# A decode-attention kernel without its block, and one semaphore for both copies of an output row

## The chip, the cores and the metric

The kernel runs on one core of a Trainium2 chip. The core has five engines that run their own instruction streams and wait for each other through semaphores: TensorE (PE in the profile; its weight loads are PEld), VectorE (DVE), ScalarE (ACT), GpSimd (POOL) and SyncE (SP). Transfers between HBM and the core's memory are issued by an engine and carried by 16 DMA engines. A semaphore is a counter: an instruction or a landed transfer adds to it, and an instruction can wait until it has reached a value.

The metric is the device time of one execution in microseconds (us). Before the change it was 247.52 us, the median of 3 runs from 247.37 to 247.62.

## The reference

Two attention layers, A and B, each with one new token, are computed on inputs of their own, and their output rows are joined. Each has 32 query heads, 16 key and value heads (so two query heads share one), 8192 cached positions and a head size of 128. Layer A looks at the last 2048 positions alone, layer B at all 8192.

```python
W = min(4096, max(256, Sk // 4))          # A: 2048
q = (x @ wq).reshape(B, Sq, Hq, Dh)...    # x: 1 x 576
k = jnp.repeat(k_cache[:, :, Sk - W:, :], rep, axis=1)      # B: the whole cache
v = jnp.repeat(v_cache[:, :, Sk - W:, :], rep, axis=1)
scores = jnp.einsum("bhqd,bhkd->bhqk", q, k) * (Dh ** -0.5)
p = _softmax(scores, axis=-1)
o = jnp.einsum("bhqk,bhkd->bhqd", p, v)
return o.transpose(0, 2, 1, 3).reshape(B, Sq, Hq * Dh) @ wo
...
return jnp.concatenate([a, b], axis=-1)   # 1 x 1 x 1152, bf16
```

## The kernel before

The work is the reading of the caches and weights, some 103 MB, each byte used once or twice. All large loads go into one ring buffer, `ring`, in a fixed order that SP issues: the query weights of both layers, then keys and values in eight units (four of layer A, four of layer B, each with four key heads), then the output weights, the last of which come in five pieces of falling size. A load into a part of the ring waits until the work that read this part before is done.

For each unit, DVE transposes the keys slab by slab (`ktb`, line 363), PE multiplies them with the queries (`score`, line 380), the maximum is taken and spread (`peak`, `spread`), ACT makes the exponentials (`expo`, line 419), DVE transposes them (`turnp`), and PE multiplies them with the values (`pv`, line 444). The transposing and scoring of the next unit are put between the softmax steps of the present one. After the last unit the sums are divided out, and the output projection (line 523) makes, for layer A and then layer B, one row of 576 numbers in two pieces of 320 and 256. ACT copies the first piece from PSUM (line 531), DVE the second (line 533), and SP sends the row out (line 535).

The program is written through the class `Prog`. Its methods `op` and `load` only append to a list for each engine; a dependency is the name of an earlier operation. An operation that others depend on adds 1 to its engine's own semaphore (`prog_act`, `prog_dve` and so on). A load adds 16 to a semaphore of its own. `emit` then walks through each engine's list and, ahead of each operation, puts a wait for every semaphore that the engine has not yet seen reach the wanted value (`eng.wait_ge`, line 83). Of several waits ahead of one instruction, the last is carried by the instruction itself and the ones before it stand as instructions of their own, which the profile shows as event semaphores.

`emit` hands each engine's list to a block: `with nc.Block() as block: pg.emit(block)`, lines 538 and 539, with a function for each of the five engines (`@block.sync` and so on). A block gives each engine a part of the program of its own, to which the engine goes from the main body. At the block's end every engine drains, adds to a common semaphore, and waits until POOL, which counts the others, lets all of them go. In the profile the instructions of the block's end stand on line 539. Those on line 554, where the program is opened, are memsets of constants and a barrier of the same kind, ahead of everything else. SP's list ends with an empty instruction that waits until both output rows have landed.

Of the kernel before, what the change touches and what calls it, by code (L numbers as in the profile page):

```python
# [8 lines left out]
ACT = mybir.ActivationFunctionType  # L9
# [5 lines left out]
DM = 576  # L15
# [14 lines left out]
N0 = 320  # L30
# [6 lines left out]
class Prog:  # L37
# [9 lines left out]
    def op(self, eng, fn, deps=(), name=None):  # L47
        self.ops[eng].append((fn, tuple(deps), name, None))
        if name is not None:
            assert name not in self.where, name  # L50
            self.where[name] = (eng, len(self.ops[eng]) - 1)

    def load(self, eng, fn, sem, value, deps=(), name=None):
        self.ops[eng].append((fn, tuple(deps), None, sem))
        if name is not None:
            assert name not in self.dma, name
            self.dma[name] = (sem, value)

    def emit(self, block):
        used = set()  # L60
        for ops in self.ops.values():
            for _, deps, _, _ in ops:
                used.update(d for d in deps if d not in self.dma)
        value = {}
        for e, ops in self.ops.items():
            n = 0
            for _, _, name, _ in ops:
                if name in used:
                    n += 1
                    value[name] = (self.sem[e], n, e)  # L70

        def run(e, eng):
            seen = {}
            for fn, deps, name, dsem in self.ops[e]:
                need = {}
                for d in deps:
                    s, v = self.dma[d] if d in self.dma else value[d][:2]
                    key = id(s)
                    if v > need.get(key, (None, 0))[1]:
                        need[key] = (s, v)  # L80
                for key, (s, v) in need.items():
                    if v > seen.get(key, 0):
                        eng.wait_ge(s, v)
                        seen[key] = v
                ins = fn(eng)
                if dsem is not None:
                    ins.then_inc(dsem, 16)
                elif name in used:
                    ins.then_inc(self.sem[e], 1)

        @block.sync
        def _(eng):
            run("sp", eng)

        @block.gpsimd
        def _(eng):
            run("pool", eng)

        @block.tensor
        def _(eng):  # L100
            run("pe", eng)

        @block.vector
        def _(eng):
            run("dve", eng)

        @block.scalar
        def _(eng):
            run("act", eng)


def bass_concat_heads__sliding_block_cached__gqa_block_cached__decode_kernel(nc, A_x, A_k_cache, A_v_cache, A_wq, A_wo,
# [47 lines left out]
    outsb = nc.alloc_sbuf_tensor("outsb", [1, 2 * DM], BF16)  # L160
# [10 lines left out]
    pg = Prog(nc)  # L171
    op, load = pg.op, pg.load
    s_x = [nc.alloc_semaphore("s_x%d" % i) for i in range(2)]
    s_ld = [nc.alloc_semaphore("s_ld%d" % i) for i in range(NSEM)]
    s_out = nc.alloc_semaphore("s_out")


    live, at, nload, uses_of = [], [0], [0], []

    def place(size, uses, issue, name):  # L180
        if at[0] + size > RING:
            at[0] = 0
        lo, hi = at[0], at[0] + size
        at[0] = hi
        deps = []
        for r in list(live):
            if r[0] < hi and lo < r[1]:
                deps += r[2]
                live.remove(r)
        n = nload[0]  # L190
        nload[0] += 1
        if n >= NSEM:
            deps += uses_of[n - NSEM]
        uses_of.append(list(uses))
        live.append((lo, hi, list(uses)))
        t = ring[:, lo:hi]
        load("sp", lambda e: issue(e, t), s_ld[n % NSEM], 16 * (n // NSEM + 1), deps=deps, name=name)
        return t
# [47 lines left out]
    def slab(kind, i, s):  # L246
# [10 lines left out]
       deps=["id0"], name="ident")  # L257
# [6 lines left out]
    for P in range(2):  # L264
        x = xs[P]
        load("act", lambda e, x=x, P=P: e.dma_start(
            xrow[0:1, P * DM:(P + 1) * DM], bass.AP(tensor=x.tensor, offset=x.offset, ap=[[DM, 1], [1, DM]])),
            s_x[P], 16, name="x%d" % P)
# [4 lines left out]
    for c in range(2):  # L273
        op("dve", lambda e, c=c: e.tensor_reduce(par[:, c:c + 1], view(identf, 128, c, [[2, 64]]), AX.X, ALU.add),
           deps=["identf"], name="par%d" % c)
# [3 lines left out]
    for P in range(2):  # L279
# [3 lines left out]
        for k in range(5):  # L283
            def mm(e, P=P, k=k):
                if k < 4:
                    lhsT = view(xrow, 2 * DM, P * DM + k, [[4, 128]], parts=1)
                else:
                    lhsT = xdup[0:1, P, :]
                return e.matmul(banks[2 * P + k // 4][:, (k % 4) * 128:(k % 4 + 1) * 128], lhsT=lhsT,  # L289
                                rhs=onesb[0:1, :], start=True, stop=True)  # L290
# [3 lines left out]
        for c in range(2):  # L294
            op("dve", lambda e, P=P, c=c: e.tensor_scalar(
                xrep[:, P, 4 + c, :], banks[2 * P + 1][:, 0:128], par[:, c:c + 1], None, ALU.mult),
                deps=["xT%d.4" % P, "par%d" % c], name="xr%d.%d" % (P, 1 + c))
# [3 lines left out]
       deps=["identf"], name="clsb")  # L301
    op("dve", lambda e: e.tensor_reduce(clsa[:], view(identf, 128, 0, [[1, 8], [8, 16]]), AX.X, ALU.add),
       deps=["identf"], name="clsa")
    op("dve", lambda e: e.tensor_reduce(sel[:], view(identf, 128, 0, [[1, 32], [32, 4]]), AX.X, ALU.add),
       deps=["identf"], name="sel")
# [6 lines left out]
    for P in range(2):  # L312
        for n in range(8):
# [3 lines left out]
            def mm(e, P=P, n=n, bank=bank):  # L317
# [8 lines left out]
               name="qmm%d.%d" % (P, n))  # L326
            op("act", lambda e, u=u, bank=bank: e.activation(qsb[:, u % 4, :], bank[:, :], ACT.Copy),  # L327
               deps=["qmm%d.%d" % (P, n)] + (["qT%d" % (u // 2 - 2)] if u >= 4 else []), name="qe%d" % u)
            if n % 2:
# [3 lines left out]
                    deps=["qe%d" % (u - 1), "qe%d" % u] + (["z0.%d" % i for i in range(4)] if P else []),  # L333
                    name="qT%d" % (u // 2))
        for b in range(4):
            if P == 1:
# [3 lines left out]
                    deps=["qT%d" % u for u in range(4, 8)] + ["zb0"], name="z1.%d" % b)  # L340
            else:
# [3 lines left out]
                    deps=["qT%d" % u for u in range(4)] + ["za0"], name="z0.%d" % b)  # L345
# [122 lines left out]
    for i in range(NU):  # L468
# [34 lines left out]
       deps=["lsel", "lselA", "nb%d" % last, "mr%d" % last], name="L")  # L503
# [3 lines left out]
        deps=["rl", "O%d" % last], name="on")  # L507
    op("dve", lambda e: e.transpose(oq[:].rearrange("p c k -> p (c k)"), on[:].rearrange("p c k -> p (c k)")),
       deps=["on"], name="oq")
# [5 lines left out]
    fb = qb[0]  # L515
    for P in range(2):
        k0 = 0
        for c, kk in enumerate(NWO[P]):
            def mm(e, P=P, c=c, k0=k0, kk=kk):
                for k in range(kk):  # L520
                    for n in range(2):
                        r, lo, hi = 32 * (2 * P + n), n * N0, N0 + n * (DM - N0)
                        ins = e.matmul(fb[r:r + 1, 0:hi - lo], lhsT=oP[:, P, k0 + k:k0 + k + 1],  # L523
                                       rhs=wo_at[P, c][:, k * DM + lo:k * DM + hi],
                                       start=(k0 + k == 0), stop=(k0 + k == HQ - 1))
                return ins
            op("pe", mm, deps=["wo%d.%d" % (P, c), "oP", "exp%d" % (NQ - 2)], name="F%d.%d" % (P, c))
            k0 += kk
        done = "F%d.%d" % (P, len(NWO[P]) - 1)
        r, lo = 64 * P, P * DM  # L530
        op("act", lambda e, r=r, lo=lo: e.activation(outsb[0:1, lo:lo + N0], fb[r:r + 1, 0:N0], ACT.Copy),
           deps=[done], name="f%d.0" % P)
        op("dve", lambda e, r=r, lo=lo: e.tensor_copy(outsb[0:1, lo + N0:lo + DM], fb[r + 32:r + 33, 0:DM - N0]),  # L533
           deps=[done], name="f%d.1" % P)
        load("sp", lambda e, lo=lo: e.dma_start(out[0, 0:1, lo:lo + DM], outsb[0:1, lo:lo + DM]),
             s_out, 16 * (P + 1), deps=["f%d.0" % P, "f%d.1" % P], name="out%d" % P)
    op("sp", lambda e: e.nop(), deps=["out1"])

    with nc.Block() as block:
        pg.emit(block)  # L540


# [26 lines left out]
```

## Time and profile before

| | before |
|---|---|
| median of 3 runs | 247.52 us (247.37 to 247.62) |
| the profiled execution | 247.68 us |
| its span, first to last instruction of the trace | 245.5 us |
| instructions | 2266 |
| PE / DVE / ACT / POOL busy | 71% / 53% / 10% / 3% of the span |
| HBM read | 102.76 MB, 419 GB/s over the span |
| mean granted TensorE clock | 0.805 |

The profile is that of one execution. Its time is longer than its span, since the execution also has parts before the first and after the last instruction of the program, which the trace does not hold. An engine's name with a q (SPq) stands for instructions that its sequencer handles alone: waits, branches, drains and the issuing of DMAs. These are not counted as busy. A row such as `L539 SPq DRAIN x1: 7/7/7, 245.3 to 245.3` gives the line, the engine, the instruction and how many, the shortest, median and longest duration in ns, and the start of the first and the last of them in us. In the chain of work and in the timeline each row begins with the start and the duration in us. In the table of waits a row gives who waited for whom, the total in us, how often, and the longest.

### The profile page before, as it was taken

Reading aid. Unit: us, or ns where it says so; the run is one execution under the profiler, and the core shown is the slowest. Engines: PE = TensorE matmul, PEld = TensorE weight load, DVE = VectorE, ACT = ScalarE, POOL = GpSimd, SP = SyncE. Lnnn points to the kernel's source line nnn. Section 1 sums busy time; section 2 is a strip of 40 time slices with the busy share of each in tenths; the row PEclk is TensorE's granted clock in tenths of the full one; section 3 lists DMA queues with packets and bytes.
Section 4 is the critical chain, followed back from the end, with each engine's and each line's share of the span. In section 5 each row is a group of like instructions: output and inputs, shape, how many; then the busy total and the mean of one; then the engine's idle time right before and its main releaser. Section 6 shows DMA issues by size and latency. Waiting matters only on the chain.

```text
span 245.5 us, 2266 instructions
## 1 busy us (share of the span) xinstructions
PE 174.3 (71%) x960; PEld 73.5 (30%) x961; DVE 129.5 (53%) x162; ACT 24.3 (10%) x52; POOL 8.2 (3%) x15
## 2 busy tenths in 40 slices
PE   0269958789769995799371979946679939338396
PEld 0124423234433323332030523212423203214263
DVE  0423447786878986799301699810689910500200
ACT  2005530101201000100000100000010000100001
POOL 8400000000000000000000000000000000000000
PEclk9999997797995999579859559977558976875569
DMA  7999999999999999998999999899999999999993
GB/s 272 415 450 413 441 430 424 427 427 456 428 435 392 472 427 427 446 470 384 406 432 435 459 448 470 384 411 440 432 460 448 406 395 435 427 444 426 412 408 144
DMA packets 4482, 102.90 MB, mean 419 GB/s; under 512 B 501, under 2 KB 633, under 8 KB 1145
## 3 DMA queue, kind: packets, MB, share of 16 engines
q1 hardware_dynamic: 4468, 102.76, 97.8%
q8 instruction: 7, 0.11, 0.2%
q14 instruction: 3, 0.02, 0.0%
q10 hardware_dynamic: 4, 0.00, 0.0%
HBM read 102.76 MB, written 0.00 MB: 419 GB/s over the span
## 4 chain that ended last, share of the span: by engine, by line
DMA 70%; PE 20%; DVE 8%; issue 1%; SPq 1%; ACT 0%; DVEq 0%
DMA ring<-in_B_v_cache_dram 39%; DMA ring<-in_B_wo_dram 13%; DMA ring<-in_B_k_cache_dram 12%; PE vb L444 8%; DVE ktb L363 7%; DMA ring<-in_A_wq_dram 5%; PE sb L323 4%; PE qb L323 3%; PE sb L380 3%; PE qb L523 1%; SPq L242 0%; PE ob L460 0%; DVE ktb L330 0%; DVE zb L337 0%; ACT qsb L327 0%
## 5 line engine op out<-in xcount | busy, mean ns | idle before, releaser
L363 DVE STREAM_TRANSPOSE ktb<-ring 128x1024 int32<-128x1024 int32 x80 | 92.9, 1212 | 30.1 <-DMA ring<-in_B_k_cache_dram 29.4
L380 PE MATMUL sb<-ktb,zb 128*128 128x512 bf16 x256 | 76.7, 445 | 21.8 <-DVE ktb L363 19.5
L380 PEld LDWEIGHTS sb<-ktb,zb 128*128 128x128 bf16 x256 | 24.1, 108 | 70.8 <-DVE ktb L363 41.8
L444 PE MATMUL vb<-ring,pts 128*32 128x512 bf16 x256 | 24.8, 568 | 20.5 <-DMA ring<-in_B_v_cache_dram 16.4
L380 PE MATMUL qb<-ktb,za 128*128 128x512 bf16 x64 | 20.2, 466 | 1.5 <-DVE ktb L363 1.5
L444 PEld LDWEIGHTS vb<-ring,pts 128*32 128x32 bf16 x256 | 8.9, 135 | 35.5 <-DMA ring<-in_B_v_cache_dram 18.5
L451 ACT ACTIVATE xo<-vb 128x512 f32<-128x512 f32 x8 | 4.8, 597 | 131.8 <-PE vb L444 131.8
L431 DVE STREAM_TRANSPOSE pts<-psb 32x512 bf16<-32x512 bf16 x16 | 11.3, 703 | 8.6 <-ACT psb L419 8.4
L330 DVE STREAM_TRANSPOSE ktb<-qsb 128x512 int32<-128x512 int32 x8 | 5.7, 711 | 14.7 <-ACT qsb L327 14.7
L323 PE MATMUL sb<-ring,xrep 128*128 128x512 bf16 x40 | 11.4, 441 | 2.9 <-DMA ring<-in_A_wq_dram 2.5
L523 PE MATMUL qb<-ring,oP 128*1 128x256 bf16 (+1 forms) x128 | 11.1, 333 | 3.0 <-DMA ring<-in_A_wo_dram 2.8
L460 PEld LDWEIGHTS ob<-sel,xo 128*128 128x128 f32 x64 | 11.6, 260 | 3.8 <-ACT xo L451 2.4
L460 PE MATMUL ob<-sel,xo 128*128 128x8 f32 x64 | 11.0, 299 | 1.2 <-ACT xo L451 1.2
L380 PEld LDWEIGHTS qb<-ktb,za 128*128 128x128 bf16 x64 | 6.4, 112 | 12.3 <-issue 6.3
L323 PE MATMUL qb<-ring,xrep 128*128 128x512 bf16 x39 | 9.1, 379 | 0.0
L523 PEld LDWEIGHTS qb<-ring,oP 128*1 128x1 bf16 x128 | 6.7, 92 | 7.3 <-DMA ring<-in_A_wo_dram 2.9
L504 DVE RECIPROCAL rl<-mb 128x64 f32<-128x64 f32 x1 | 0.6, 558 | 14.0 <-PE mb L501 14.0
L533 DVE CAST outsb<-qb 1x256 bf16<-1x256 f32 x2 | 0.8, 420 | 13.4 <-PE qb L523 13.4
L289 PE MATMUL sb<-onesb,xrow 1*128 1x128 bf16 x4 | 0.6, 295 | 9.2 <-DVE xdup L280 9.2
L405 DVE TENSOR_REDUCE mr<-mb 1x8 f32<-1x128 f32 x8 | 1.9, 241 | 9.4 <-PE mb L397 9.4
L323 PEld LDWEIGHTS sb<-ring,xrep 128*128 128x128 bf16 x40 | 4.2, 108 | 8.9 <-issue 5.6
L327 ACT ACTIVATE qsb<-sb 128x512 bf16<-128x512 f32 x8 | 4.8, 598 | 19.2 <-PE sb L323 18.5
(65 smaller groups left out, 69.5 us busy)
## 6 DMA issues: line engine op xcount, KB each, us to landing
ring<-in_B_k_cache_dram SPq DMA_DIRECT2D x8, 4096.0 KB, 25.3
ring<-in_A_k_cache_dram SPq DMA_DIRECT2D x4, 2048.0 KB, 30.9
ring<-in_A_v_cache_dram SPq DMA_DIRECT2D x4, 2048.0 KB, 26.2
ring<-in_B_v_cache_dram SPq DMA_DIRECT2D x2, 4096.0 KB, 24.1
ring<-in_A_wo_dram SPq DMA_DIRECT2D x1, 4608.0 KB, 24.4
ring<-in_A_wq_dram SPq DMA_DIRECT2D x1, 4096.0 KB, 12.4
ring<-in_B_wq_dram SPq DMA_DIRECT2D x1, 4096.0 KB, 22.4
ring<-in_B_wo_dram SPq DMA_DIRECT2D x1, 2448.0 KB, 29.9
```

The lines of the kernel that those rows point to most:

```text
L323: ins = e.matmul(bank[:, :], lhsT=lhsT, rhs=o, start=(k == 0), stop=(k == 4))
L327: op("act", lambda e, u=u, bank=bank: e.activation(qsb[:, u % 4, :], bank[:, :], ACT.Copy), deps=["qmm%d.%d" % (P, n)] + (["qT%d" % (u // ...
L330: op("dve", lambda e, u=u, n=n: e.transpose(ktb[:, (n - 1) * 512:(n + 1) * 512].bitcast(I32), qsb[:, u % 4 - 1:u % 4 + 1, :].rearrange("p ...
L363: op("dve", lambda e: e.transpose(kt.bitcast(I32), src.bitcast(I32)), deps=[landed] + (["S%d" % (k - NKT)] if k >= NKT else Z), name="T%d. ...
L380: ins = e.matmul(bank[:, :], lhsT=lhsT, rhs=view(ktb, KT, (k % NKT) * SLAB + 64 * c + v, [[128, 16], [2, 32]]), start=(side == "B" and s = ...
L405: op("dve", lambda e: e.tensor_reduce(out, view(mb, 512, 0, rows, parts=1), AX.X, ALU.max), deps=deps, name="mr%d" % i)
L431: op("dve", lambda e, b=b: e.transpose(view(pts, NB * 128, 2 * b, [[8, 16], [128, NB], [1, 2]], 32, 32 * b), psb[32 * b:32 * b + 32, :]), ...
L444: ins = e.matmul(vbank[i][32 * j:32 * j + 32, :], lhsT=lhsT, rhs=src[:, 512 * j:512 * j + 512], start=(s == 0), stop=(s == nslab[i] - 1))
L451: op("act", lambda e: e.activation(xo[:, c, :], vbank[i][:, :], ACT.Copy), deps=["V%d.%d" % (i, nslab[i] - 1)] + (["O%d" % (i - 1)] if i e ...
L460: ins = e.matmul(ob[:, at:at + 8], lhsT=xo[:, c, 128 * t:128 * t + 128], rhs=sel[:, 8 * t:8 * t + 8], start=(t == 0), stop=(t == 3))
L523: ins = e.matmul(fb[r:r + 1, 0:hi - lo], lhsT=oP[:, P, k0 + k:k0 + k + 1], rhs=wo_at[P, c][:, k * DM + lo:k * DM + hi], start=(k0 + k == 0 ...
L533: op("dve", lambda e, r=r, lo=lo: e.tensor_copy(outsb[0:1, lo + N0:lo + DM], fb[r + 32:r + 33, 0:DM - N0]), deps=[done], name="f%d.1" % P)
```

## The change

There are two parts. The block is gone: `emit` calls the same function for each engine in turn on the engines of the main body, so that the instructions follow the opening barrier directly and nothing of the block's end stands behind them. SP's list ends with a wait alone: an operation without a function puts out its waits and nothing more. And the two copies of an output row, one by ACT and one by DVE, each add 1 to a semaphore of that row, `s_row[P]`; the row's DMA waits for the value 2, where it waited for DVE's and for ACT's own semaphore.

```diff
-    def load(self, eng, fn, sem, value, deps=(), name=None):
-        self.ops[eng].append((fn, tuple(deps), None, sem))
+    def load(self, eng, fn, sem, value, deps=(), name=None, step=16):
+        self.ops[eng].append((fn, tuple(deps), None, (sem, step)))
...
-    def emit(self, block):
+    def emit(self):
...
+                if fn is None:
+                    continue
                 ins = fn(eng)
                 if dsem is not None:
-                    ins.then_inc(dsem, 16)
+                    ins.then_inc(*dsem)
...
-        @block.sync
-        def _(eng):
-            run("sp", eng)
-
-        @block.gpsimd
-        def _(eng):
-            run("pool", eng)
...
+        for e, eng in (("sp", self.nc.sync), ("pool", self.nc.gpsimd), ("pe", self.nc.tensor),
+                       ("dve", self.nc.vector), ("act", self.nc.scalar)):
+            run(e, eng)
...
+    s_row = [nc.alloc_semaphore("s_row%d" % i) for i in range(2)]
...
-        op("act", lambda e, r=r, lo=lo: e.activation(outsb[0:1, lo:lo + N0], fb[r:r + 1, 0:N0], ACT.Copy),
-           deps=[done], name="f%d.0" % P)
-        op("dve", lambda e, r=r, lo=lo: e.tensor_copy(outsb[0:1, lo + N0:lo + DM], fb[r + 32:r + 33, 0:DM - N0]),
-           deps=[done], name="f%d.1" % P)
+        load("act", lambda e, r=r, lo=lo: e.activation(outsb[0:1, lo:lo + N0], fb[r:r + 1, 0:N0], ACT.Copy),
+             s_row[P], 2, deps=[done], name="f%d" % P, step=1)
+        load("dve", lambda e, r=r, lo=lo: e.tensor_copy(outsb[0:1, lo + N0:lo + DM], fb[r + 32:r + 33, 0:DM - N0]),
+             s_row[P], 2, deps=[done], step=1)
         load("sp", lambda e, lo=lo: e.dma_start(out[0, 0:1, lo:lo + DM], outsb[0:1, lo:lo + DM]),
-             s_out, 16 * (P + 1), deps=["f%d.0" % P, "f%d.1" % P], name="out%d" % P)
-    op("sp", lambda e: e.nop(), deps=["out1"])
-
-    with nc.Block() as block:
-        pg.emit(block)
+             s_out, 16 * (P + 1), deps=["f%d" % P], name="out%d" % P)
+    op("sp", None, deps=["out1"])
+
+    pg.emit()
```

More of the change, by code (lines that the diff above doesn't have):

```diff
@@ L84, in run @@
                         seen[key] = v
+                if fn is None:
+                    continue
                 ins = fn(eng)
                 if dsem is not None:
-                    ins.then_inc(dsem, 16)
+                    ins.then_inc(*dsem)
                 elif name in used:
                     ins.then_inc(self.sem[e], 1)
-        @block.sync
-        def _(eng):
-            run("sp", eng)
-        @block.gpsimd
-        def _(eng):
-            run("pool", eng)
[L99 to L109, printed above, removed]
+        for e, eng in (("sp", self.nc.sync), ("pool", self.nc.gpsimd), ("pe", self.nc.tensor),
+                       ("dve", self.nc.vector), ("act", self.nc.scalar)):
+            run(e, eng)
 def bass_concat_heads__sliding_block_cached__gqa_block_cached__decode_kernel(nc, A_x, A_k_cache, A_v_cache, A_wq, A_wo,
```

## The prediction

> **What bounds the kernel now.** I read the busy line and the slices first, then the DMA queues, the chain that ended last, the records of the two lines outside the work (554, where the program is opened, and 539, where the block ends), and SP's waits.
>
> ```profile
> span 245.5 us, 2266 instructions
> PE 174.3 (71%) x960; PEld 73.5 (30%) x961; DVE 129.5 (53%) x162; ACT 24.3 (10%) x52; POOL 8.2 (3%) x15
> DMA  7999999999999999998999999899999999999993
> HBM read 102.76 MB, written 0.00 MB: 419 GB/s over the span
> ```
>
> No engine is busy for much more than 71% of the span, while the DMA engines are full in all slices but the first and the last. The kernel reads 102.76 MB and is bound by that reading. The change touches no load, so it can only act on the two ends, where the DMA engines are not full: the start, before the first load is under way, and the end, after the last load has landed. The chain of work shows both.
>
> ```profile
> 0.67 0.06 issue
> 0.73 0.41 SPq L205
> 1.14 0.06 issue
> 1.20 13.18 DMA ring<-in_A_wq_dram
> ...
> 36.57 4.64 DVE ktb L363 x4
> 41.20 0.02 issue
> 41.22 29.23 DMA ring<-in_B_k_cache_dram
> ...
> 92.14 1.01 PE vb L444 x16
> 93.15 0.02 issue
> 93.17 0.02 SPq L83
> 93.18 0.03 issue
> 93.21 30.75 DMA ring<-in_B_v_cache_dram
> ...
> 242.86 0.66 PE qb L523 x5
> 243.51 0.02 issue
> 243.54 0.43 ACT outsb L531
> ```
>
> SP issues the first load at 0.73. At the other end PE's last product of the output projection is done at 243.51 and the copy of the second output row at 243.54 + 0.43 = 243.97. The chain is cut there, but the span goes on to 245.5: 1.5 us for the output's DMA and the end of the program.
>
> ```profile
> 244.04 0.25 SPq L535 DMA_DIRECT2D out_dram<-outsb  x1
> ...
> SPq L539 <- DMA out_dram<-outsb: 0.9, 1, 0.9
> SPq L539 <- PEq L539: 0.2, 1, 0.2
> ```
>
> The DMA is issued from 244.04 to 244.29. SP waits 0.9 us for its landing, so to about 245.2, and then for the barrier of the block's end.
>
> **The change part by part.** First the end of the block. The records of line 539, asked for whole and then for SP in narrow windows, are these (the second fence holds SP's branch from the window 245.15 to 245.17 us, its drain from 245.31 to 245.33, and, from 245.47 to 245.54, the event semaphores of SP and PE, with those of ACT and DVE between them left out).
>
> ```profile
> L539 POOLq DRAIN  x1: 7346/7346/7346, 1.6 to 1.6; - x1
> L539 PEldq DRAIN  x1: 355/355/355, 243.2 to 243.2; - x1
> L539 ACTq DRAIN  x1: 459/459/459, 243.5 to 243.5; - x1
> L539 DVEq DRAIN  x1: 464/464/464, 243.6 to 243.6; - x1
> ```
>
> ```profile
> L539 SPq COMPARE_BRANCH  x1: 33/33/33, 245.2 to 245.2; - x1
> ...
> L539 SPq DRAIN  x1: 7/7/7, 245.3 to 245.3; - x1
> ...
> L539 SPq EVENT_SEMAPHORE  x1: 17/17/17, 245.5 to 245.5; - x1
> ...
> L539 PEldq EVENT_SEMAPHORE  x1: 51/51/51, 245.5 to 245.5; - x1
> ```
>
> The drains of the other four engines are over before 244.1 (243.6 + 0.46 at the latest), under the output's DMA: they cost nothing. SP is the last to come, and all that follows its branch is on the path: the branch at 245.16, the drain 0.16 later at 245.32, POOL's count of the others, and the release, which ends with PE's event semaphore (0.051) that begins at 245.47 or after. So the span ends between 245.52 and 245.55, 0.36 to 0.39 us after the branch began. In the changed kernel SP ends with a bare wait for the output's semaphore. Its price is that of the same kind of instruction in the row above, 0.017. The end of the block thus gives 0.36 us.
>
> [...]
>
> Second, the semaphore of the row. Now SP needs two waits ahead of the row's DMA: a standalone one for DVE's copy (line 83) and one carried by the DMA for ACT's.
>
> ```profile
> L83 SPq EVENT_SEMAPHORE  x6: 17/17/17, 53.0 to 244.0; - x6
> ```
>
> With both copies counting on one semaphore the DMA carries the only wait. Two loads in the chain above price the two forms. With a standalone wait first, PE ends at 93.15 and the load begins at 93.21, 0.06 later; with a carried wait alone, DVE ends at 41.20 (36.57 + 4.64) and the load begins at 41.22, 0.02 later. Here it is 243.97 to 244.04, 0.07. So the second row's DMA starts 0.04 to 0.05 earlier; I take 0.04. The first row's is earlier by as much, which is worth nothing: SP has nothing to do after it until the second row comes. The copies themselves keep their engine, order and size, and nothing is queued behind them.
>
> Third, the start. A block has each engine branch from the main body into its own part. If that cost time it would stand between the opening barrier and the first instruction. The chain shows 0.06 of issue time ahead of the first load at 0.73, and the same 0.06 ahead of the next load, with no branch between. So the price is 0, with 0.06 as the upper bound. No queue gets its instructions in another order; the loads stay SP's, and the two small ones ACT's.
>
> Fourth, what lies outside the span. The profiled execution took 247.68 us, so 2.14 to 2.18 us of it are not in the trace. Now all five engines come out of the block at the same moment, 245.5, and enter what follows together. After the change POOL, PE, DVE and ACT run on without a barrier once their own work is done, by 244.1 at the latest, and SP alone comes at 245.1. If the others need longer than SP for what follows, that excess is now hidden. Nothing in the trace shows it; it is bounded by 0 and by the whole 2.14. The nearest rows are those of the same five engines on the way in, which start together from outside and reach their first instruction at different times.
>
> ```profile
> L554 SPq DRAIN  x1: 7/7/7, 0.0 to 0.0; - x1
> L554 DVEq DRAIN  x1: 10/10/10, 0.1 to 0.1; - x1
> L554 POOLq INC_SWDGE_SEM  x1: 27/27/27, 0.1 to 0.1; - x1
> L554 ACTq DRAIN  x1: 8/8/8, 0.1 to 0.1; - x1
> ...
> L554 POOLq DRAIN  x1: 186/186/186, 0.3 to 0.3; - x1
> ...
> L554 PEldq DRAIN  x1: 8/8/8, 0.3 to 0.3; - x1
> ```
>
> SP is the first and PE the last, 0.3 later. If PE lags as much on the way out, 0.3 us go with the barrier. I take 0.3 as an estimate from these two rows.
>
> Sum: 0.36 + 0.04 = 0.40 us inside the span, which goes from 245.5 to 245.1, and 0.3 outside. The profiled execution goes from 247.68 to 246.98. It stands 0.16 above the median of 247.52, so the forecast for the median is 247.52 - 0.70 = 246.82, rounded to 246.8, 0.3% faster. I count 0.2% (0.5 us) as what a measurement of this kernel can tell from no change.
>
> **The rivals.**
>
> *Only the span shrinks: 247.1.* What follows the program may begin only when the last engine has arrived, or SP may be the slowest there. Then the other engines' early arrival buys nothing and the gain is 0.40: 247.12, 0.16%, within 0.2%. For it: SP already comes last before the change. Against it: nothing that the trace shows. [...]
>
> *More is hidden outside: 246.0.* If the four engines' own ends are most of the 2.14 us, some 1.1 us could go (half of it, as an estimate between the bounds): 247.52 - 0.40 - 1.1 = 246.0. Against it: the lag on the way in is only 0.3.
>
> *Nothing goes: 247.5.* The program may get a barrier at its end all the same, put there when it is closed, as one stands at its opening on line 554. Then only the 0.04 of the row remains, 247.5. For it: an opening barrier is there without the program asking for one. Against it: all end records bear line 539, the block's own; none is left for a second barrier.
>
> *The table load moves ahead of the opening barrier: 248.0, slower.* ACT's first instruction in the block loads its function table.
>
> ```profile
> L263 ACT ACT_TABLE_LOAD  x1: 1283/1283/1283, 0.7 to 0.7; - x1
> ```
>
> With one body for each engine, this load could be placed at the head of it, before ACT's drain of the opening barrier. That drain, at 0.1 now, would come at 0.1 + 1.28 = 1.4, where the last of the others, PE's, comes at 0.3. POOL's own memsets and drain hold the barrier until about 0.5 (its drain starts at 0.3 and takes 0.186), so the barrier and SP's first load would be 0.9 us later. The loads bound the kernel from there on, so all of it reaches the end: 247.52 + 0.9 - 0.40 = 248.0, and 247.7 if the 0.3 outside goes too. It decides against the change once the first load starts later than 0.73 + 0.40 = 1.13. For it: all instructions now stand in one body, so its head is at the barrier. Against it: the load is needed only by the first activation, on line 263, and stands directly before it now.
>
> **How the numbers follow.** The forecast case, 0.1 to 0.5 us hidden outside (246.6 to 247.0), gets 0.45; the span alone 0.22; more hidden 0.12; nothing 0.06; the table load, with whatever else could delay the start, 0.15. The two gains of over 0.5 us sum to 0.57, and a tenth of the span-alone case, where it lies near the bound, makes 0.59 faster; the rest of it and nothing gone make 0.26 within 0.2%; slower is 0.15. The predicted time is 246.8, the likeliest case. The range goes from 246.0, the middle of the case of more hidden, to 247.6, just above nothing gone; left out are the lower half of the former and the slower case, 2 in 10.
>
> **What the changed profile would show.** No records of a block's end; SP's last one is a wait for the output's semaphore near 245.1, and it ends the span. Of SP's six standalone waits the two ahead of the output's DMAs are gone, and the last output DMA begins 0.02 to 0.03 after the copies. The first load is still issued at 0.73; if it is at 1.6, the table load moved. The difference between execution time and span is 2.14 now: near 1.9 it bears out the forecast, unchanged the first rival, near 1.1 the second. The prediction is wrong if the opening changes, if a barrier comes back at the end, or if the engines that run on alone hold up what follows.

## The result and the profile after

| | before | after |
|---|---|---|
| median | 247.51 us (6 runs, 247.37 to 247.62) | 246.28 us (6 runs, 246.09 to 246.60) |
| ratio | | 0.9952, 95% interval 0.9942 to 0.9962 |
| the profiled execution | 247.68 us | 246.60 us |
| its span | 245.5 us | 245.2 us |
| its time outside the span | 2.14 us | 1.35 us |

By the medians the kernel is 1.23 us faster; the ratio puts it at 0.48%. The forecast was 0.70 us, the range 246.0 to 247.6.

The page of the changed kernel shows the same work as before, with 13 instructions fewer (2266 before):

```profile
span 245.2 us, 2253 instructions
PE 172.3 (70%) x960; PEld 71.8 (29%) x961; DVE 129.1 (53%) x162; ACT 24.3 (10%) x52; POOL 8.2 (3%) x15
DMA  7999999999999999998999999999999999999994
HBM read 102.76 MB, written 0.00 MB: 419 GB/s over the span
```

The start is the same. The chain of work has the rows of before to the hundredth:

```profile
0.67 0.06 issue
0.73 0.41 SPq L192
```

ACT's drain in the opening barrier (line 541 now) and its table load (line 250 now) stand where they stood, which their records give to the tenth:

```profile
L541 ACTq DRAIN  x1: 8/8/8, 0.1 to 0.1; - x1
```

```profile
L250 ACT ACT_TABLE_LOAD  x1: 1283/1283/1283, 0.7 to 0.7; - x1
```

The end is shown by the timeline's rows of the second output row, SP's DMA, SP's waits from 244 us on, and SP's wait instruction on line 83 in the window 245.22 to 245.25 us:

```profile
243.65 0.43 ACT L519 ACTIVATE outsb<-qb 1x320 bf16<-1x320 f32 x1 [3.47 <-PE qb L510]
243.65 0.43 DVE L521 CAST outsb<-qb 1x256 bf16<-1x256 f32 x1 [3.49 <-PE qb L510]
```

```profile
244.11 0.25 SPq L523 DMA_DIRECT2D out_dram<-outsb  x1
```

```profile
SPq L523 <- ACT outsb L519: 3.6, 1, 3.6
SPq L83 <- DMA out_dram<-outsb: 0.9, 1, 0.9
```

```profile
L83 SPq EVENT_SEMAPHORE  x1: 17/17/17, 245.2 to 245.2; - x1
```

The DMA follows the copies by 0.03 us (243.65 + 0.43 = 244.08, then 244.11) where it took 0.07, and SP's wait for its landing is the last instruction of the program. No row of a block's end is left. In this one execution the last copies began at 243.65, 0.11 later than the 243.54 in the one shown of before, so its span shrank by less than the end did. Averaged over executions, the span goes from 245.38 us (27 runs of the kernel before, those beside the first experiments below) to 244.97 us (6 runs of the changed one), 0.41 less. Time minus span, taken run by run and averaged (the spans are given to 0.1 us, so a mean is good to some 0.03), goes from 2.15 to 1.34 us, 0.81 less. So two thirds of the gain lie where the trace has no instruction.

### The profile page after: what moved, and what is told of

The parts are those of the page before. It is cut to its first block, busy times and chain, and to the rows that moved or that the text cites. A ratio compares the mean times of both kernels' runs of the same rounds, so it can differ in the third digit from the quotient of the medians.

```text
span 245.2 us, 2253 instructions
## 1 busy us (share of the span) xinstructions
PE 172.3 (70%) x960; PEld 71.8 (29%) x961; DVE 129.1 (53%) x162; ACT 24.3 (10%) x52; POOL 8.2 (3%) x15
## 4 chain that ended last, share of the span: by engine, by line
DMA 55%; PE 29%; DVE 12%; ACT 2%; issue 2%; SPq 0%; DVEq 0%
DMA ring<-in_B_v_cache_dram 40%; DMA ring<-in_A_wo_dram 10%; DVE ktb L350 9%; PE vb L431 8%; DMA ring<-in_A_wq_dram 5%; PE qb L367 5%; PE qb L510 5%; PE sb L310 5%; PE qb L310 4%; ACT psb L406 1%; DVE pta L414 1%; PE ob L447 1%; PE sb L367 1%; PE qb L359 1%; PE mb L397 1%
## 5 line engine op out<-in xcount | busy, mean ns | idle before, releaser
L367 PEld LDWEIGHTS sb<-ktb,zb 128*128 128x128 bf16 x256 | 23.4, 106 | 72.4 <-DVE ktb L350 45.9
L367 PE MATMUL qb<-ktb,za 128*128 128x512 bf16 x64 | 19.4, 449 | 2.8 <-DVE ktb L350 2.8
L447 PEld LDWEIGHTS ob<-sel,xo 128*128 128x128 f32 x64 | 10.9, 244 | 3.8 <-ACT xo L438 2.2
L447 PE MATMUL ob<-sel,xo 128*128 128x8 f32 x64 | 10.1, 285 | 1.2 <-ACT xo L438 1.2
```

The costliest lines, as they stand in the source:

```text
L367: ins = e.matmul(bank[:, :], lhsT=lhsT, rhs=view(ktb, KT, (k % NKT) * SLAB + 64 * c + v, [[128, 16], [2, 32]]), start=(side == "B" and s = ...
L447: ins = e.matmul(ob[:, at:at + 8], lhsT=xo[:, c, 128 * t:128 * t + 128], rhs=sel[:, 8 * t:8 * t + 8], start=(t == 0), stop=(t == 3))
```

## The experiments

Where does the gain outside the span come from? Theory 1: the other four engines now go through what follows their own program before SP comes, where before all five began it together. Theory 2: a program that ends in its main body costs less outside than one that ends in a block's end. A third possibility is that the row's semaphore does more than it shows. Differences below are in us of the medians, each to the kernel before as it ran beside the variant, since that kernel's median lay between 247.51 and 247.58 from one occasion to another. "Outside" is time minus span, averaged over a kernel's runs.

### The two parts of the change alone

The block stays, and only the row's semaphore is shared, so that the row's DMA has one wait (against the kernel before, lines cut short at the dots):

```diff
-    def load(self, eng, fn, sem, value, deps=(), name=None):
-        self.ops[eng].append((fn, tuple(deps), None, sem))
+    def load(self, eng, fn, sem, value, deps=(), name=None, step=16):
+        self.ops[eng].append((fn, tuple(deps), None, (sem, step)))
...
-        op("act", ..., name="f%d.0" % P)
-        op("dve", ..., name="f%d.1" % P)
+        load("act", ..., s_row[P], 2, deps=[done], name="f%d" % P, step=1)
+        load("dve", ..., s_row[P], 2, deps=[done], step=1)
```

> The block stays; only the two copies of an output row count on one semaphore. Both theories expect little: the row's DMA starts 0.04 us sooner, so the time is that of the kernel before less 0.04 us (about 247.5), the span 245.5, and the time outside the span stays at 2.14 us. If instead the row's semaphore carries the gain, the time is near 246.3.

Measured: 247.47 against 247.53, ratio 0.9997 (0.9989 to 1.0006). Outside the span 2.15.

The block goes, and the copies keep their two semaphores and the row's DMA its two waits (against the changed kernel, cut short in the same way):

```diff
-        load("act", ..., s_row[P], 2, deps=[done], name="f%d" % P, step=1)
-        load("dve", ..., s_row[P], 2, deps=[done], step=1)
+        op("act", ..., name="f%d.0" % P)
+        op("dve", ..., name="f%d.1" % P)
```

> The block is gone; the copies of an output row keep their two semaphores and SP its two waits. If the block's end is the whole of it: 0.04 us above the changed kernel, so about 246.3, with 1.35 us outside the span. If the row's semaphore carries the gain: near 247.5 less the 0.36 us of the barrier, 247.1.

Measured: 246.32 against 247.53, ratio 0.9951 (0.9938 to 0.9965). Outside the span 1.31.

The block's end carries the gain. The row's share (0.06 in the one pair, 1.23 less 1.21 in the other) is not told from zero by these times; its 0.04 is seen in the trace alone.

### The changed kernel with what the block's end did, piece by piece

First, all five engines wait for the output's landing, with no barrier:

```diff
-    op("sp", None, deps=["out1"])
+    for q in ("sp", "pool", "pe", "dve", "act"):
+        op(q, None, deps=["out1"])
```

> The changed kernel, but POOL, PE, DVE and ACT also wait for the landing of the output at their ends, as SP does; no barrier, no drain, no branch. Theory 1 (the gain outside the span is that the other four engines arrive early at what follows the program): all five arrive together again, so the time outside the span goes back from 1.35 to 2.1 us, the span hardly changes (PE's wait ends 0.05 us after SP's), and the time is near 246.28 + 0.8 = 247.1. Theory 2 (the gain outside comes from leaving the program from the main body and not from a block's end): outside stays at 1.35 us and the time at 246.3.

Measured: 247.05 against 247.53, ratio 0.9982 (0.9973 to 0.9991). Outside the span 2.05. Its wait instructions on line 83 in the window 245.1 to 245.3 us:

```profile
L83 SPq EVENT_SEMAPHORE  x1: 17/17/17, 245.1 to 245.1; - x1
L83 ACTq EVENT_SEMAPHORE  x1: 17/17/17, 245.2 to 245.2; - x1
L83 POOLq EVENT_SEMAPHORE  x1: 17/17/17, 245.2 to 245.2; - x1
L83 DVEq EVENT_SEMAPHORE  x1: 21/21/21, 245.2 to 245.2; - x1
L83 PEldq EVENT_SEMAPHORE  x1: 51/51/51, 245.2 to 245.2; - x1
```

Four short waits, in the shadow of SP's but for PE's 0.05, put 0.75 us on the time (1.23 less 0.48), 0.71 of it outside the span (2.05 less 1.34). There is no block here, so theory 2 can't carry the 0.81: at most the 0.10 between 2.05 and the 2.15 of before is left to it. What counts is when the engines arrive.

Second, a barrier over all engines behind the last instruction, in the main body:

```diff
     pg.emit()
+    nc.all_engine_barrier()
```

> The changed kernel with the library's barrier over all engines put behind the last instruction, in the main body and without a block. Theory 1: the block's end without its branch; the span gets about 0.25 us longer (drain of SP, POOL's count, release), outside goes back to 2.1 us, and the time is near 247.4. Theory 2: the span gets longer by the same 0.25 us but outside stays at 1.35 us: 246.55.

Measured: 247.37 against 247.53, ratio 0.9993 (0.9985 to 1.0002). Outside the span 2.14, as with the block's end, though this program ends in its main body: the rest of the way to 2.15 is there with the barrier and without the block, and theory 2 falls. SP's wait on line 83, in the window 244.99 to 245.01 us, and its drain in the barrier on line 528, in the window 245.05 to 245.07:

```profile
L83 SPq EVENT_SEMAPHORE  x1: 17/17/17, 245.0 to 245.0; - x1
```

```profile
L528 SPq DRAIN  x1: 7/7/7, 245.1 to 245.1; - x1
```

Here the drain comes 0.06 after the wait, where in the kernel before it came 0.16 after the start of the branch: in these two executions the branch, which carries the wait, took 0.10 more than the wait alone.

The steps from the kernel before to the changed one are then: 0.16 for the branch and the row's semaphore (247.53 to 247.37), 0.32 for the barrier (to 247.05; mean spans 245.23 and 245.01), and 0.75 for the early arrival of four engines (to 1.23 below the kernel before). The first of them is not told from zero by the times alone, since its ratio's interval holds 1; the rows give 0.10 for the branch and 0.04 for the row's semaphore.

### Which engine is slow outside

The changed kernel, with one engine waiting for the landing beside SP, and then with that engine alone waiting, so that SP is done when it has issued the last DMA:

```diff
-    op("sp", None, deps=["out1"])
+    for q in ("sp", "act"):        # then "dve", "pool", "pe"; and each of the four without "sp"
+        op(q, None, deps=["out1"])
```

Beside SP:

> The changed kernel, with PE alone also waiting for the landing of the output at its end, beside SP. Theory 1a (one engine is slow in what follows the program, and by the order of the first instructions that is PE): nearly all of the 0.77 us between 246.28 and 247.05 comes back here, so 247.0 and 2.1 us outside the span. Theory 1b (what follows is a chain through the engines, and each late engine adds its own share): a quarter, 0.2 us, so 246.5. Theory 1c (the cost is in other engines than PE): 246.3.

> The same with ACT as the one that waits beside SP. Theory 1a with PE as the slow one: 246.3, nothing comes back. Theory 1b: 246.5. If ACT is the slow one: 247.0.

> The same with DVE as the one that waits beside SP. Theory 1a with PE as the slow one: 246.3. Theory 1b: 246.5. If DVE is the slow one: 247.0.

> The same with POOL as the one that waits beside SP. Theory 1a with PE as the slow one: 246.3. Theory 1b: 246.5. If POOL is the slow one: 247.0.

Alone:

> The changed kernel, but ACT waits for the landing of the output at its end in place of SP; SP is done once it has issued the last DMA, 0.9 us before. Theory A (each engine needs a time of its own after its last instruction, and the slowest of the late ones sets the end): ACT beside SP gave 0.3 us more than SP alone, so ACT is the slower of the two and alone gives the same, 246.6. Theory B (the late engines hinder each other, or are served one after the other, so their number counts): one late engine is as good as another, 246.3.

> The same with DVE alone waiting for the output. Theory A: as beside SP, 246.6. Theory B: 246.3.

> The same with POOL alone waiting for the output. Theory A: as beside SP, 246.8. Theory B: 246.3.

> The same with PE alone waiting for the output. Theory A: as beside SP, 246.7. Theory B: 246.3, or 0.05 more for PE's longer wait instruction.

| late engine | beside SP: median, against before | outside | alone: median, against before | outside |
|---|---|---|---|---|
| SP (the changed kernel) | | | 246.28, -1.23 | 1.34 |
| ACT | 246.58, -1.00 | 1.48 | 246.43, -1.08 | 1.48 |
| PE | 246.78, -0.80 | 1.58 | 246.62, -0.89 | 1.59 |
| DVE | 246.66, -0.92 | 1.65 | 246.61, -0.90 | 1.66 |
| POOL | 246.87, -0.71 | 1.87 | 246.80, -0.71 | 1.87 |
| all five | 247.05, -0.48 | 2.05 | | |

The ratios run from 0.9957 (ACT alone, 0.9943 to 0.9971) to 0.9974 (POOL alone, 0.9963 to 0.9984) for the single engines. The kernel before had a median of 247.58 beside the left half, 247.53 beside the run with all five and 247.51 beside the right half.

None of the theories stated ahead of the left half holds as it stood. They were: PE is the one slow engine and brings nearly all of the 0.75 back (1a), each engine adds a share of its own to a chain (1b), or PE brings nothing back (1c). PE brought back 0.43 us of the 1.23, ACT 0.23, DVE 0.31 and POOL 0.52. So PE is neither the only one nor without part, and the four sum to 1.49, twice the 0.75 that shares would add up to. The right half was forecast by theory A, and three of its four times came within 0.1 us of it; ACT's, 246.43 for 246.6, did not, but its time outside did, at 1.48 in both halves: the runs of ACT beside SP had a mean span of 245.16, those of ACT alone 244.96.

In the execution with POOL beside SP both waits stand within the window 244.8 to 245 us, and with POOL alone its own is the only one from 244.8 to 245.3:

```profile
L83 SPq EVENT_SEMAPHORE  x1: 17/17/17, 244.9 to 244.9; - x1
L83 POOLq EVENT_SEMAPHORE  x1: 17/17/17, 244.9 to 244.9; - x1
```

```profile
L83 POOLq EVENT_SEMAPHORE  x1: 17/17/17, 244.9 to 244.9; - x1
```

The time outside is the same whether SP is late too or not: 1.48 and 1.48 for ACT, 1.58 and 1.59 for PE, 1.65 and 1.66 for DVE, 1.87 and 1.87 for POOL. So theory A holds for one late engine beside SP: each engine needs a time of its own behind its last instruction, and the slower of the two late ones sets the end. If the number of late engines counted (theory B), the single ones would all be near 1.34. SP is the quickest of the five and POOL the slowest, by 0.53 us. In the profiled execution of the changed kernel the last copies of ACT and DVE end at 244.08 and SP's wait at 245.25, so these engines are 1.17 us ahead of SP, and PE and POOL more (PE's last product ends at 243.63, POOL's last work at 8.93): longer than any of these differences.

Theory A alone doesn't give the 2.05 of all five, which lies 0.18 above POOL's 1.87. What the engines do there is in no trace, so why the times differ, and whether several late engines hinder each other, or one must wait for another there, stay open. No variant here beats the changed kernel: the one engine that it leaves to the end is the quickest.

## Why the prediction was right, and where it was too small

**The block's end, 0.36, and the row, 0.04.** Right: 0.40 was forecast inside the span, and the mean span fell by 0.41. The drains of the other four engines cost nothing, as said: in the kernel before they are over by 244.1, and SP's branch comes at 245.16. The row's DMA starts 0.03 after the copies (forecast 0.02 to 0.03). Of the 0.16 from SP's branch to its next instruction, 0.06 is there behind a plain wait too, in the run with the end barrier.

**The start, 0.** Right: SP's first load is issued at 0.73 in both, and ACT's table load is still at 0.7. The slower rival, by which that load moves ahead of the opening barrier, did not come about.

**Outside the span, 0.3.** The mechanism was right and the size was not: the term measured 0.81, and it is the whole of the 0.5 us by which the forecast was short. By the forecast's own signs this is not its likeliest case, which had 0.1 to 0.5 hidden and some 1.9 left: the 1.34 is nearer to the 1.1 of "more is hidden". The result lies in the range because the range left room for that rival, which had a chance of 0.12. The estimate failed in its rows. I took the lag of the engines on the way in, with SP first and PE last by 0.3, for their lag on the way out; no row shows that they start together there, or that the two are alike. On the way out PE lags by 0.24 (1.58 less 1.34), close to that, which may be chance, but POOL lags by 0.53, and all together by 0.71 (2.05 less 1.34). POOL's first record on the way in, at 0.1, gave no sign of it. The measured 0.81 is higher than 0.71 by the rest that the barrier has outside (2.15 against 2.05).

**The rivals.** "Only the span shrinks", 247.1, is met by the kernel in which all five engines wait: 247.05. That is the changed kernel without its early arrivals, so the rival priced the rest nearly rightly (0.40 for 0.48) and erred in holding that early arrival buys nothing. Whether something behind the program waits for all engines, no run here shows; but the time outside depends on which engine comes last, from 1.34 with SP to 1.87 with POOL, so the last arrival alone does not fix the time, where the rival held that it may. "More is hidden", with 1.1 at 246.0, was on the other side of the truth: 0.81 lies between it and the forecast, nearer to the rival. Its condition, that the four engines' own ends are most of the 2.14, did not hold: 0.81 is under two fifths. "Nothing goes" fell: the trace has no barrier at the end.

## What to carry to other kernels

Time and span are two numbers, and a change at the end of a program can act on what lies between them: here 0.81 us, where the span gave 0.41. Let engines whose work is done leave: a wait of all five for the last transfer cost 0.75 us here, 0.71 of it outside the span, and the barrier over them 0.32 more. If one engine must stay for the last landing, leave it to the one with the shortest way out, here SP (1.34 us outside, against 1.48 to 1.87 with another).

## What the runs showed of the hardware

Time minus span depends on which engine ends last: it was 1.34 us with SP, 1.48 with ACT, 1.59 with PE, 1.66 with DVE and 1.87 with POOL, the same with SP late beside it to within 0.02, and 2.05 with all five. These figures also hold whatever lies ahead of the first instruction, which no run here tells apart; the programs differ only at their ends, so it is the differences between the figures that belong there. A branch of SP with a wait on it took 0.10 us more than the wait alone: 0.16 from its start to SP's next instruction in the kernel before, 0.06 in the run with the end barrier.
